# First batch of a fused attention and MLP kernel: where fills, transposes and global queries stand

## The chip, the cores and the metric

The kernel runs on one core of one Trainium2 chip. The metric is the device time of one execution in microseconds (us). Every time of a whole kernel quoted here is a median, with the range beside it where it matters; events within a kernel come from one profiled execution each.

The engines are called PE (TensorE matmul), DVE (VectorE), ACT (ScalarE), Pool (GpSimd) and SP (SyncE, which here only issues loads and stores).

## The reference

Eight batches, eight heads, 512 local and 32 global positions, head size 64. Local queries see a window of 32 positions to each side and the 32 global keys; global queries see everything. The result goes through an MLP with a hard-swish.

```python
k_all = concat([k_g, k_l]);  v_all = concat([v_g, v_l])
out_g = softmax(scale * q_g @ k_all.T) @ v_all
s_l   = concat([scale * q_l @ k_g.T, where(|i-j| <= 32, scale * q_l @ k_l.T, -1e9)])
out_l = softmax(s_l) @ v_all
x = concat([out_g, out_l])  -> 4352 rows x 512
h = x @ w_in;  g = h * clip(h + 3, 0, 6) / 6;  out = g @ w_out
```

## The kernel before

Heads are taken in pairs: four pairs per batch, 32 pairs in all; pairs 0 to 3 are batch 0, pairs 4 to 7 batch 1. A pair goes through these steps. `cast` turns the loaded f32 tiles into f16. `emit_T`, written T(p), transposes q and k on PE and copies them out of PSUM, where PE's results lie. `emit_S`, S(p, 0) and S(p, 1), makes local scores and their exponentials. `emit_SG` and `emit_PG` are the scores and value products of the global queries. `emit_AV` and `emit_X` are the local value products and their transposes. The MLP consists of units: 16 of `u1` per batch (four matmuls with w_in each) and 16 of `u2` (four matmuls with w_out each). `M(n)` issues the next n units.

From batch 2 on, eight units of the batch before fill the gaps of each pair. This change is about what comes before: batch 0, whose weights are still being loaded, and batch 1.

All loads but those of v_g go through 13 staging buffers, used in turn. Such a load can start only when the cast of the tile 13 loads earlier has emptied its buffer.

```python
    NSTG = 13
    def emit_T(p):                       # one PSUM tile for k and q
        psT = ps_tile("psT", FP16)
        for i, t in enumerate((s["kn"], s["qn"])):
            for j in range(NT):
                nc.tensor.matmul(out=psT[:, i * Sl + j * P:...], lhsT=t[:, j], rhs=ident, is_transpose=True)
        nc.vector.tensor_copy(out=kT..., in_=psT[:, 0:Sl]...)
        nc.scalar.copy(out=qT..., in_=psT[:, Sl:2 * Sl]...)
        nc.vector.tensor_copy(out=qT[:, 0:W], in_=qT[:, Sl:Sl + W])
    # ... cut ...
    def first(p):
        cast(p, "k", nc.vector);  cast(p, "qv", nc.gpsimd);  vshift(p, nc.gpsimd)
    first(0); emit_T(0); emit_G(0, 1, "kg"); kglob(0, nc.vector)
    for p in range(NM):                  # NM = 4 pairs of batch 0
        emit_S(p, 0, True)
        if p >= 2: emit_X(p - 2)
        if p + 1 < NM: first(p + 1); emit_T(p + 1)
        if p >= 1: emit_AV(p - 1)
        emit_S(p, 1, True)
    # ... u1 of units 0 to 3, casts of w_in on Pool ...
    nc.gpsimd.memset(qgz, 0.0)           # the fills, all on Pool
    nc.gpsimd.memset(vgs[0], 0.0); nc.gpsimd.memset(vgs[0][rg, :, D:P], 1.0)
    nc.gpsimd.memset(vts[0][:, :, :, D:P], 1.0)
    # ... vgs[0] copy, Eg ...
    for c in range(4, 12): u1(c)
    emit_G(0, 4, "qg"); emit_G(1, 4, "kg")
    for p in range(NM):                  # global queries inside the first MLP
        u1(12 + p); emit_SG(p)
        if p: emit_PG(p - 1)
    emit_PG(NM - 1)
    pin(*ALL)                            # program order up to here, on every engine
    emit_XG(0)
    fill_v(1, nc.gpsimd)                 # ... more fills of batch 1 on Pool ...
    for b in range(1, B): load_vg(b)     # seven v_g loads, issued by Pool
    for i in range(NC): cast_w("out", i, nc.gpsimd)
    kglob(1, nc.gpsimd); vglob(1, nc.gpsimd)
    for p in range(NM, 2 * NM): cast(p, "kqv", nc.gpsimd); vshift(p, nc.gpsimd)
    M(6); emit_T(4); M(1); emit_S(4, 0); M(1); emit_T(5); emit_S(4, 1); emit_SG(4)
```

The softmax here doesn't subtract the row's maximum and nothing guards it: scores larger than these inputs give would overflow.

## Time and profile before

362.3 us (361.7 to 364.3, 4 runs); the profiled execution spans 361.0 us. Four parts of the profile carry the argument. First the page's slices: 40 equal slices of 9 us, each digit the busy share in tenths; PEclk is the granted PE clock in tenths of full speed.

```profile
PE   0778589699999999999999999999999999999994
...
POOL 4756999996840067006710562055300000000000
PEclk9999969589999999999999999999999999999999
DMA  8999299999950669055903590259211000100202
```

From about 100 us on PE is full: it is the bound there, and a pair takes 9.36 us. Before that there are gaps. The stage table gives them in us; its columns are the stretch, its length, busy us (and instructions) of PE, of PE's weight loads, DVE, ACT and Pool, then granted clock, DMA share and GB/s.

```profile
0.00:9.00 9.00, 0.72 (x8) 0.73 (x8) 5.05 (x17) 1.28 (x1) 4.41 (x14) 1.00 0.86 211
...
36.00:45.00 9.00, 4.86 (x25) 2.01 (x22) 7.27 (x9) 4.12 (x6) 8.71 (x13) 0.95 0.22 79
45.00:54.00 9.00, 7.42 (x70) 4.04 (x71) 3.53 (x8) 4.47 (x11) 8.96 (x17) 0.67 0.97 205
...
63.00:72.00 9.00, 5.94 (x59) 3.56 (x59) 6.29 (x12) 5.41 (x11) 8.57 (x15) 0.59 0.96 225
```

In 36 to 45 us Pool is full, the DMA engines do 0.22 of what they could, and PE is half idle. The chain of waits (start, length, what) says why:

```profile
24.62 6.85 DMA stg<-in_moe_w_in_dram
31.52 0.61 POOL win L169
...
32.79 1.75 POOL qgz L464
...
36.05 1.81 POOL vt L467
...
38.98 1.80 POOL vb L418
...
41.06 1.70 POOL vt L484
...
44.40 3.94 POOL vg L150 x7
...
48.39 6.50 POOL wout L169 x12
...
57.98 2.27 POOL vb L145 x4
...
60.88 0.61 POOL kn L136
```

From 31.5 to 61.5 us the chain is one run on Pool: fills from 32.7 to 44.4, v_g issues, w_out casts, copies, then the first casts of batch 1. While the fills run, the full staging buffers of w_out wait for their casts, so no load can start.

Lastly two pairs of lines of the timeline (start, length, engine, line, operation, out<-in; in brackets the idle time before and what ended it). The k and q copies of T(0) don't overlap, and PE waits for the cast of the global queries' rows, which took 2.23 us on DVE:

```profile
9.35 0.69 DVE L215 COPY kT<-psT 128x512 f16<-128x512 f16 x1 [1.13 <-PE psT L209]
10.07 0.58 ACT L218 COPY qT<-psT 128x512 f16<-128x512 f16 x1 [7.97 <-DVE kT L215]
...
41.71 2.23 DVE L185 CAST qgn<-stg 128x512 f16<-128x512 f32 x1
44.00 0.51 PE L188 MATMUL psGT<-ident,qgn 128*128 128x128 f16 x4 [3.65 <-DVE qgn L185]
```

### The profile page before, as it was taken

What the parts mean: (1) busy time and instruction counts of PE and PEld (TensorE: products, weight loads), DVE (VectorE), ACT (ScalarE), POOL (GpSimd) and SP (SyncE); (2) the same over time, 40 slices, a digit from 0 to 9 for tenths busy, and PEclk for the clock granted to TensorE, in tenths of its full rate; (3) what the DMA queues carried; (4) which work ended last, traced back from release to release, by engine and by line L of the source; (5) the groups of instructions that cost most, each with busy time, mean ns of one, the idle gap of its engine ahead of it and who ended that gap; (6) DMA issues with size and microseconds to landing.
All of it is one profiled execution on the core that took longest, in us unless ns stands there. A gap on an engine that the chain in (4) does not pass through costs nothing.

```text
span 361.0 us, 7891 instructions
## 1 busy us (share of the span) xinstructions
PE 331.7 (92%) x3044; PEld 175.4 (49%) x3044; DVE 230.3 (64%) x522; ACT 208.6 (58%) x434; POOL 138.2 (38%) x229
## 2 busy tenths in 40 slices
PE   0778589699999999999999999999999999999994
PEld 0344244355455555555555555555555555544472
DVE  5465832688888468746885589458855786375070
ACT  1464451557885478746874587558845883284170
POOL 4756999996840067006710562055300000000000
PEclk9999969589999999999999999999999999999999
DMA  8999299999950669055903590259211000100202
GB/s 211 335 240 344 74 209 296 224 171 202 192 104 3 146 156 169 2 132 139 197 3 95 139 225 12 59 137 230 44 32 59 31 2 29 60 29 6 84 31 58
DMA packets 103845, 44.29 MB, mean 123 GB/s; under 512 B 91264, under 2 KB 95360, under 8 KB 103808
## 3 DMA queue, kind: packets, MB, share of 16 engines
q1 hardware_dynamic: 101632, 43.53, 51.4%
q0 software_dynamic: 2176, 0.26, 1.2%
q8 instruction: 24, 0.39, 0.5%
q14 instruction: 13, 0.11, 0.1%
HBM read 35.13 MB, written 8.91 MB: 122 GB/s over the span
## 4 chain that ended last, share of the span: by engine, by line
PE 71%; POOL 8%; DVE 6%; DMA 5%; ACT 4%; SPq 3%; issue 1%; POOLq 0%; DVEq 0%; ACTq 0%
PE po L359 30%; PE psH L343 25%; PE psS L243 5%; DMA stg<-in_moe_w_in_dram 4%; PE psT L209 3%; POOL wout L169 2%; DVE E L249 2%; PE psX L316 2%; ACT E L247 2%; SPq L120 2%; PE pav L286 2%; PE pav L283 2%; PE psSG L260 2%; DMA stg<-in_v_l_dram 2%; ACT t L348 1%
## 5 line engine op out<-in xcount | busy, mean ns | idle before, releaser
L359 PE MATMUL po<-wout,gt 128*128 128x512 f16 x544 | 128.1, 382 | 0.0
L343 PE MATMUL psH<-xt,win 128*128 128x512 f16 x512 | 122.0, 384 | 0.6 <-DVE xt L320 0.5
L350 DVE SCALAR_TENSOR_TENSOR gt<-t,psH 128x512 f16<-128x512 f32 (+1 forms) x144 | 90.7, 653 | 30.1 <-ACT t L348 29.1
L348 ACT ACTIVATE t<-psH,half_col 128x512 f32<-128x512 f32 (+1 forms) x144 | 91.5, 669 | 29.7 <-PE psH L343 28.2
L247 ACT ACTIVATE E<-psS 128x512 f16<-128x512 f32 x128 | 70.3, 613 | 22.4 <-PE psS L243 21.9
L343 PEld LDWEIGHTS <-win 128*128 128x128 f16 x576 | 53.1, 98 | 51.2 <-issue 2.4
L359 PEld LDWEIGHTS <-gt 128*128 128x128 f16 x544 | 49.6, 98 | 53.4 <-issue 1.3
L249 DVE TENSOR_TENSOR E<-E,mk 128x512 f16<-128x512 f16 x112 | 55.0, 504 | 29.1 <-ACT E L247 27.1
L145 POOL COPY vb<-vg 32x512 f16<-32x512 f16 x28 | 16.6, 631 | 72.9 <-PE pav L286 72.7
L363 ACT COPY ot<-po 128x512 f32<-128x512 f32 x17 | 10.0, 586 | 57.5 <-PE po L359 57.5
L243 PEld LDWEIGHTS <-kT 64*128 64x128 f16 x512 | 15.5, 97 | 30.4 <-issue 26.0
L243 PE MATMUL psS<-qT,kT 64*128 64x128 f16 x512 | 27.2, 227 | 3.3 <-DVE qT L220 3.2
L320 DVE COPY xt<-psX 128x512 f16<-128x512 f16 x32 | 13.4, 420 | 22.6 <-PE psX L316 22.5
L292 DVE TENSOR_TENSOR xn<-pav,rc 128x256 f16<-128x256 f32 x64 | 26.5, 421 | 1.4
L136 POOL CAST vt<-stg 128x512 f16<-128x512 f32 x32 | 20.4, 638 | 12.3 <-DMA stg<-in_v_l_dram 10.8
L136 POOL CAST qn<-stg 128x512 f16<-128x512 f32 x32 | 20.7, 646 | 7.5 <-DMA stg<-in_q_l_dram 7.0
L136 POOL CAST kn<-stg 128x512 f16<-128x512 f32 x28 | 17.5, 625 | 14.8 <-DMA stg<-in_k_l_dram 13.7
L363 DVE COPY ot<-po 128x512 f32<-128x512 f32 x17 | 11.6, 685 | 17.1 <-PE po L359 17.1
L209 PE MATMUL psT<-ident,kn 128*128 128x128 f16 x128 | 13.2, 228 | 9.6 <-DVE kn L136 9.3
L141 POOL COPY vb<-vt 64x512 f16<-64x512 f16 x32 | 20.7, 646 | 2.1
L224 ACT COPY qT<-psT 128x512 f16<-128x512 f16 x24 | 14.0, 583 | 12.9 <-DVE kT L222 12.9
L286 PE MATMUL pav<-vb,E 128*128 128x65 f16 x256 | 20.2, 195 | 0.0
(76 smaller groups left out, 314.9 us busy)
## 6 DMA issues: line engine op xcount, KB each, us to landing
stg<-in_k_l_dram SPq DMA_DIRECT2D x32, 256.0 KB, 4.8
stg<-in_q_l_dram SPq DMA_DIRECT2D x32, 256.0 KB, 4.9
stg<-in_v_l_dram SPq DMA_DIRECT2D x32, 256.0 KB, 4.9
out_dram<-ot SPq DMA_DIRECT2D x24, 256.0 KB, 2.2
stg<-in_moe_w_in_dram SPq DMA_DIRECT2D x16, 256.0 KB, 5.1
stg<-in_moe_w_out_dram SPq DMA_DIRECT2D x16, 256.0 KB, 5.3
out_dram<-ot SPq DMA_DIRECT2D x8, 192.0 KB, 2.2
out_dram<-ot SPq DMA_DIRECT2D x16, 64.0 KB, 1.9
```

Source lines behind the costliest of these rows:

```text
L136: eng.tensor_copy(out=o, in_=s[c + "f"])
L209: nc.tensor.matmul(out=psT[:, i * Sl + j * P:i * Sl + (j + 1) * P], lhsT=t[:, j], rhs=ident, is_transpose=True)
L243: nc.tensor.matmul(out=pss[e][:, w * P:(w + 1) * P], lhsT=kT[r, c0:c0 + P], rhs=qT[r, w * P:(w + 1) * P], start=not pe_mask, stop=True, sk ...
L247: nc.scalar.activation(out=E[:, ch, e], in_=pss[e], func=EXP, scale=qk_scale)
L249: nc.vector.tensor_tensor(out=E[:, ch, e], in0=E[:, ch, e], in1=mk[:, ch].rearrange("p w c -> p (w c)"), op=mult)
L286: nc.tensor.matmul(out=o, lhsT=E[:, 1, e, w * P:(w + 1) * P], rhs=vb[:, (w - 1) % NT, h, 0:D + 1], start=False, stop=True, skip_group_chec ...
L292: nc.vector.tensor_tensor(out=xn[:, 2 * w2:2 * w2 + 2].rearrange("p w (e d) -> p w e d", e=2), in0=pv[:, :, :, 0:D], in1=rc.to_broadcast([ ...
L343: nc.tensor.matmul(out=ps[:, 0:n], lhsT=w_in_t[m][:, c * P:(c + 1) * P], rhs=rhs(m), start=(m == 0), stop=(m == NM - 1), skip_group_check= ...
L348: nc.scalar.activation(out=t1[:, 0:n], in_=ps[:, 0:n], func=RELU, bias=half_col, scale=1.0 / 6.0)
L350: nc.vector.scalar_tensor_tensor(out=gts[c][:, 0:n], in0=t1[:, 0:n], scalar=1.0, in1=ps[:, 0:n], op0=amin, op1=mult)
L359: nc.tensor.matmul(out=po[t][:, 0:dm], lhsT=gts[c][:, t * P:(t + 1) * P], rhs=w_out_t[c // 4][:, c % 4], start=(c == 0), stop=(c == NC - 1))
L363: (nc.scalar.copy if t % 2 else nc.vector.tensor_copy)(out=ot, in_=po[t][:, 0:dm])
```

## The change

Its intent: take the fills out of Pool's queue, so that w_out and batch 1 are cast as they land; let the copies of q and k overlap by giving each a PSUM bank of its own (a bank is the part of PSUM that one tile fills here); run all transposes of batch 0 as early as the data allows; and put batch 0's global queries behind the w_out casts. The diff, cut to its core:

```diff
-    def emit_T(p):
+    def emit_T(p, qdve=False):
-        psT = ps_tile("psT", FP16)
-        for i, t in enumerate((s["kn"], s["qn"])):
+        ps = {}
+        for c in "kq":
+            ps[c] = ps_tile("psT" + c, FP16)[:, 0:Sl]
             for j in range(NT):
                 ... transposes ...
+        qcopy = nc.vector.tensor_copy if qdve else nc.scalar.copy
@@ loads
     for i in range(NC):
         load_w("in", i)
-        if i == 7:
-            load_g(0, 4, "qg"); load_g(1, 4, "kg")
     for i in range(NC):
         load_w("out", i)
+        if i == 3:
+            load_g(1, 4, "kg"); load_g(0, 4, "qg")
@@ fills: ones_v on ACT, the others on DVE, all but vgs[1]
+    fill_v(0, nc.vector); ones_v(0); nc.scalar.memzero(qgz)
+    cast(0, "k", nc.vector)             # in front of the mask work
     ... mneg built straight from mb, mk later from mneg ...
+    for p in range(1, NM): first(p)     # casts k, q and v, all on Pool
+    for i in range(NC): cast_w("in", i, nc.gpsimd)
+    emit_S(0, 0, True); emit_T(1, True); emit_S(0, 1, True); emit_T(2)
+    emit_S(1, 0, True); emit_S(1, 1, True); emit_AV(0); emit_T(3, True)
+    emit_S(2, 0, True); emit_X(0); ...
     HEAD = 3
     ... u1 of units 0 to 2 spread between AV and X ...
+    fill_vg(0, nc.vector); ... Eg on DVE ...
     for c in range(HEAD, NC): u1(c)     # no global queries in between
     for i in range(NC): cast_w("out", i, nc.gpsimd)
+    emit_G(1, 4, "kg"); emit_G(0, 4, "qg")
+    fill_v(1, nc.vector); fill_vg(1, nc.gpsimd)
     kglob(1, nc.gpsimd); vglob(1, nc.gpsimd)
     for p in range(NM, 2 * NM):
-        cast(p, "kqv", nc.gpsimd); vshift(p, nc.gpsimd)
+        cast(p, "k", nc.vector); cast(p, "qv", nc.gpsimd); vshift(p, nc.gpsimd)
-    M(6); emit_T(4); M(1); emit_S(4, 0); M(1); emit_T(5); emit_S(4, 1); emit_SG(4)
+    M(3); pin(*ALL); emit_T(4); emit_SG(0); emit_SG(1); M(1); emit_SG(2); emit_SG(3)
+    emit_S(4, 0); M(1); (emit_PG of 0 to 3); emit_T(5); emit_S(4, 1)
+    ones_v(1); emit_SG(4); emit_XG(0)
+    for b in range(2, B): load_vg(b)
@@ batch 1's pairs
-        n = (0, 1, 0, 1) if b == 1 else (1, 2, 2, 3)
+        n = (1, 1, 0, 0) if b == 1 else (1, 2, 2, 3)
```

More of the change, by code (lines that the diff above doesn't have):

```diff
@@ L136, in cast, with vshift @@
             eng.tensor_copy(out=o, in_=s[c + "f"])
-    def vshift(p, eng):
+    def vshift(p, eng, n=1):
         b, m = divmod(p, NM)
-        hs = slice(2 * m, 2 * m + 2)
+        hs = slice(2 * m, 2 * m + 2 * n)
         eng.tensor_copy(out=vbs[b % NV][0:D, :, hs, 0:D], in_=vts[b % NV][D:P, :, hs, 0:D])
@@ L201, in kglob @@
                         in_=kgT[:, :, b].unsqueeze(2).to_broadcast([P, NM, NT, Sg]))
-    def emit_T(p):
+    def emit_T(p, qdve=False):
         b, m = divmod(p, NM)
         s = st[p]
-        psT = ps_tile("psT", FP16)
-        for i, t in enumerate((s["kn"], s["qn"])):
-            for j in range(NT):
-                nc.tensor.matmul(out=psT[:, i * Sl + j * P:i * Sl + (j + 1) * P],
-                                 lhsT=t[:, j], rhs=ident, is_transpose=True)
         kT = kTs[b % 2][:, m]
@@ L213, in emit_T @@
         qT = wrk.tile([P, Sl + W], FP16, tag="qT", name="qT", bufs=4)
+        ps = {}
+        for c in "kq":
+            ps[c] = ps_tile("psT" + c, FP16)[:, 0:Sl]
+            for j in range(NT):
+                nc.tensor.matmul(out=ps[c][:, j * P:(j + 1) * P], lhsT=s[c + "n"][:, j], rhs=ident,
+                                 is_transpose=True)
+        qcopy = nc.vector.tensor_copy if qdve else nc.scalar.copy
         if b < NRUN:
@@ L216, in emit_T @@
                 out=kv[:, :, 0:P].rearrange("p u (i j) -> p u i j", j=NT),
-                in_=psT[:, 0:Sl].rearrange("p (j u i) -> p u i j", j=NT, u=NT))
-            nc.scalar.copy(out=qT[:, W:Sl + W].rearrange("p (i j) -> p i j", j=NT),
-                           in_=psT[:, Sl:2 * Sl].rearrange("p (j i) -> p i j", j=NT))
+                in_=ps["k"].rearrange("p (j u i) -> p u i j", j=NT, u=NT))
+            qcopy(out=qT[:, W:Sl + W].rearrange("p (i j) -> p i j", j=NT),
+                  in_=ps["q"].rearrange("p (j i) -> p i j", j=NT))
             nc.vector.tensor_copy(out=qT[:, 0:W], in_=qT[:, Sl:Sl + W])
@@ L222, in emit_T @@
             nc.vector.tensor_copy(out=kv[:, :, 0:P],
-                                  in_=psT[:, 0:Sl].rearrange("p (u c) -> p u c", u=NT))
-            nc.scalar.copy(out=qT[:, W:Sl + W], in_=psT[:, Sl:2 * Sl])
-            nc.scalar.copy(out=qT[:, 0:W], in_=psT[:, 2 * Sl - W:2 * Sl])
+                                  in_=ps["k"].rearrange("p (u c) -> p u c", u=NT))
+            qcopy(out=qT[:, W:Sl + W], in_=ps["q"])
+            qcopy(out=qT[:, 0:W], in_=ps["q"][:, Sl - W:Sl])
         s["qT"], s["kT"] = qT, kT
@@ L394 @@
         load_w("in", i)
-        if i == 7:
-            load_g(0, 4, "qg")
-            load_g(1, 4, "kg")
     for i in range(NC):
         load_w("out", i)
+        if i == 3:
+            load_g(1, 4, "kg")
+            load_g(0, 4, "qg")
     for p in range(NM, 2 * NM + 1):
         load(p)
+    make_identity(nc, ident)
     load_vg(0)
-    make_identity(nc, ident)
     mb = const("mb", [P, 2, P])
-    nc.vector.memset(mb, 1.0)
-    nc.vector.memset(mb[D + Sg:P, 1], 0.0)
-    nc.gpsimd.affine_select(out=mb[:, 0], in_=mb[:, 0], compare_op=is_ge, fill=0.0,
+    ones = const("ones", [P, 1])
+    nc.vector.memset(ones, 1.0)
+    nc.vector.memset(mb, 0.0)
+    nc.vector.memset(mb[D + Sg:P, 1], -30000.0)
+    fill = -30000.0
+    nc.gpsimd.affine_select(out=mb[:, 0], in_=mb[:, 0], compare_op=is_ge, fill=fill,
                             base=0, pattern=[[1, P]], channel_multiplier=-1)
-    nc.gpsimd.affine_select(out=mb[:, 0], in_=mb[:, 0], compare_op=is_ge, fill=0.0,
+    nc.gpsimd.affine_select(out=mb[:, 0], in_=mb[:, 0], compare_op=is_ge, fill=fill,
                             base=2 * W, pattern=[[-1, P]], channel_multiplier=1)
-    nc.gpsimd.affine_select(out=mb[0:D, 1], in_=mb[0:D, 1], compare_op=is_ge, fill=0.0,
+    nc.gpsimd.affine_select(out=mb[0:D, 1], in_=mb[0:D, 1], compare_op=is_ge, fill=fill,
                             base=0, pattern=[[-1, P]], channel_multiplier=1)
@@ L419, in fill_v @@
         eng.memset(vbs[i][0:P - W, :, :, D:D + 1], 1.0)
-    fill_v(0, nc.vector)
-    nc.vector.memset(vts[0][:, :, :, D:D + 1], 1.0)
-    vglob(0, nc.vector)
-    nc.vector.tensor_copy(out=mk, in_=mb.unsqueeze(2).to_broadcast([P, 2, NT, P]))
-    nc.vector.memset(mk[:, 0, 0, 0:W], 0.0)
-    nc.vector.memset(mk[0:D, 1, 0, W:P], 0.0)
-    nc.vector.tensor_scalar(out=mneg, in0=mk.rearrange("p c w q -> p c (w q)"), scalar1=30000.0,
-                            scalar2=-30000.0, op0=mult, op1=mybir.AluOpType.add)
@@ L430, in first, with ones_v, fill_vg @@
-    def first(p):
+        eng.memset(vts[i][:, :, :, D:D + 1], 1.0)
+    def ones_v(i):
+        for u in range(NT):
+            nc.scalar.copy(out=vts[i][:, u, :, D + 1:P],
+                           in_=ones.unsqueeze(2).to_broadcast([P, H, D - 1]))
+    def fill_vg(i, eng):
+        eng.memset(vgs[i], 0.0)
+        eng.memset(vgs[i][rg, :, D:P], 1.0)
+    fill_v(0, nc.vector)
+    ones_v(0)
+    nc.scalar.memzero(qgz)
+    cast(0, "k", nc.vector)
+    mv = mneg.rearrange("p c (w q) -> p c w q", w=NT)
@@ new lines, with first @@
+    nc.vector.tensor_copy(out=mv, in_=mb.unsqueeze(2).to_broadcast([P, 2, NT, P]))
+    nc.vector.memset(mv[:, 0, 0, 0:W], fill)
+    nc.vector.memset(mv[0:D, 1, 0, W:P], fill)
+    def first(p, what="kqv"):
+        cast(p, what, nc.gpsimd)
+        vshift(p, nc.gpsimd)
+    first(0, "qv")
+    load_vg(1)
+    emit_T(0)
+    emit_G(0, 1, "kg")
+    kglob(0, nc.vector)
+    vglob(0, nc.vector)
+    units += moe_units(lambda mm: xts[0][mm], Sl, local_dests(0), early=True)
+    u1 = units.pop(0)
@@ new lines @@
+    for p in range(1, NM):
+        first(p)
+    for i in range(NC):
+        cast_w("in", i, nc.gpsimd)
+    emit_S(0, 0, True)
+    emit_T(1, True)
+    emit_S(0, 1, True)
+    emit_T(2)
+    emit_S(1, 0, True)
+    emit_S(1, 1, True)
+    emit_AV(0)
+    emit_T(3, True)
+    emit_S(2, 0, True)
+    emit_X(0)
+    emit_S(2, 1, True)
+    emit_AV(1)
+    emit_S(3, 0, True)
+    emit_X(1)
+    emit_S(3, 1, True)
+    emit_AV(2)
+    HEAD = 3
+    for c in range(HEAD):
+        u1(c, range(2))
@@ new lines @@
+    emit_X(2)
+    emit_AV(3)
+    for c in range(HEAD):
+        u1(c, range(2, 3))
+    emit_X(3)
+    for c in range(HEAD):
+        u1(c, range(3, 4))
+    fill_vg(0, nc.vector)
+    nc.vector.tensor_copy(out=vgs[0][rg, :, 0:D], in_=vg[rg, 0])
+    for t in Egs:
+        nc.vector.memset(t[:, NT], 0.0)
+    nc.vector.tensor_scalar(out=mk.rearrange("p c w q -> p c (w q)"), in0=mneg, scalar1=-1.0,
+                            scalar2=1.0, op0=is_ge, op1=mult)
+    for c in range(HEAD, NC):
+        u1(c)
@@ L431, in first @@
+    for i in range(NC):
+        cast_w("out", i, nc.gpsimd)
+    emit_G(1, 4, "kg")
+    emit_G(0, 4, "qg")
+    fill_v(1, nc.vector)
+    fill_vg(1, nc.gpsimd)
+    kglob(1, nc.gpsimd)
+    vglob(1, nc.gpsimd)
+    for p in range(NM, 2 * NM):
         cast(p, "k", nc.vector)
@@ L433, in first @@
         vshift(p, nc.gpsimd)
-    first(0)
-    emit_T(0)
-    emit_G(0, 1, "kg")
-    kglob(0, nc.vector)
-    units += moe_units(lambda mm: xts[0][mm], Sl, local_dests(0), early=True)
-    u1 = units.pop(0)
-    for p in range(NM):
-        emit_S(p, 0, True)
-        if p >= 2:
-            emit_X(p - 2)
-        if p + 1 < NM:
-            first(p + 1)
-            emit_T(p + 1)
-        if p >= 1:
-            emit_AV(p - 1)
-        emit_S(p, 1, True)
-    for i in range(4):
-        cast_w("in", i, nc.gpsimd)
-    emit_X(NM - 2)
-    HEAD = 3
-    for c in range(HEAD):
-        u1(c, range(NM - 1))
-    emit_AV(NM - 1)
-    emit_X(NM - 1)
-    for c in range(HEAD):
-        u1(c, range(NM - 1, NM))
-    u1(HEAD)
-    for i in range(4, NC):
-        cast_w("in", i, nc.gpsimd)
-    nc.gpsimd.memset(qgz, 0.0)
-    nc.gpsimd.memset(vgs[0], 0.0)
-    nc.gpsimd.memset(vgs[0][rg, :, D:P], 1.0)
-    nc.gpsimd.memset(vts[0][:, :, :, D:P], 1.0)
-    nc.gpsimd.tensor_copy(out=vgs[0][rg, :, 0:D], in_=vg[rg, 0])
-    for t in Egs:
-        nc.gpsimd.memset(t[:, NT], 0.0)
-    for c in range(4, 12):
-        u1(c)
-    emit_G(0, 4, "qg")
-    emit_G(1, 4, "kg")
-    for p in range(NM):
-        u1(12 + p)
-        emit_SG(p)
-        if p:
-            emit_PG(p - 1)
-    emit_PG(NM - 1)
-    pin(*ALL)
-    emit_XG(0)
-    fill_v(1, nc.gpsimd)
-    nc.gpsimd.memset(vts[1][:, :, :, D:P], 1.0)
-    nc.gpsimd.memset(vgs[1], 0.0)
-    nc.gpsimd.memset(vgs[1][rg, :, D:P], 1.0)
-    for b in range(1, B):
-        load_vg(b)
-    for i in range(NC):
-        cast_w("out", i, nc.gpsimd)
-    kglob(1, nc.gpsimd)
-    vglob(1, nc.gpsimd)
-    for p in range(NM, 2 * NM):
-        cast(p, "kqv", nc.gpsimd)
-        vshift(p, nc.gpsimd)
-    M(6)
+    M(3)
+    pin(*ALL)
     emit_T(4)
-    M(1)
+    emit_SG(0)
+    emit_SG(1)
+    M(1)
+    emit_SG(2)
+    emit_SG(3)
     emit_S(4, 0)
     M(1)
+    for p in range(NM):
+        emit_PG(p)
     emit_T(5)
     emit_S(4, 1)
+    ones_v(1)
     emit_SG(4)
+    emit_XG(0)
+    for b in range(2, B):
+        load_vg(b)
     for p in range(NM, NPAIR):
```

## The prediction

> **What bounds it now.** From about 110 us on TensorE is the bound: the slices show PE at 9 tenths, and the chain of waits runs through psH/po matmuls with a pair every 9.36 us. The loss lies before it: by the stage table PE is busy 0.7 us of the first 9, 4.9 of 36-45, 5.9 of 63-72. In the chain of waits, 31.5 to 61.5 us is one run on Pool: last w_in casts, 11.6 us of fills (qgz, vgs, vt, vb, Eg, 32.7-44.4), 4.0 us of v_g issues, 16 w_out casts (48.4-57.3), 4 us of copies, then the first cast of batch 1 at 60.9. The fills hold the staging buffers: DMA share falls to 0.22 in 36-45, against about 1.0 around it. PE also waits 5.1 us for the two global transposes near 44-46, and the granted clock falls to 0.59. The Trainium skill ("TensorE: Matmul & The Clock Gate", part 1) says that PE's clock is halved after idle windows; the trace agrees.
>
> **What the change does.**
> - Fills leave Pool: about 9 us of the 11.6 go to DVE, Scalar or before the loads; six v_g issues (3.4 us) go behind batch 1's casts; four k casts of batch 1 (2.4 us) go to DVE.
> - k3 was cast on DVE behind attention (21.1 us), which held back w_in's ninth load (issued 20.8) and gave Pool a 3.2 us wait. On Pool at about 14 us it doesn't. k_g/q_g loads move back.
> - q and k transposes share a bank now: the ACT copy starts at 10.07, when the DVE copy (9.35 + 0.69) ends. Own banks let them overlap: about 0.6 us per pair. ("PSUM — Partial Sum Buffer", bank collisions, says that two engines mustn't read one bank together.)
> - k0 is cast before the v_g copies and mask work: T(0) near 5.5-6 us instead of 8.3. Attention still awaits batch 0's last loads (14.9).
> - SG/PG of batch 0 run after T(4): 3 us of PE and ACT work, partly in gaps.
> - u2 units before batch 2 fall from 16 to 13; three (4 x 216 ns each, 2.6 us) go to the PE-bound stage.
>
> **Estimate.** w_in is cast near 28 us (now 32.8), batch 0's u1 ends near 34-37 (now 53), PE then waits for w_out, which comes at about 335 GB/s: cast by about 42 (now 57.3). Then 5 us of fills and copies: q4 cast at 47-48; k7 lands at 47-50, and in DVE's order T(4)'s copy waits for it. It comes near 49, not 62.5: 13 us. Batch 1's iterations stay at about 5 us (DVE: masks, copies), plus about 1 us for SG/PG; pair 8's stage begins near 78-79 instead of 91. Less 2.6 us for the three units: about 10 us net.
>
> Predicted 352.5 us (347 to 358). Faster by over 2%: 0.75; within 2%: 0.24; slower: 0.01.
>
> **Signs.** DMA share near 1 through 36-45; w_out casts end 40-44; T(4)'s kT copy 47-51; k and q copies of one pair overlap; the steady pair still 9.36 us.
>
> **What would make it wrong.** Batch 1's loads or DVE's k casts, in order, stall T(4) past 53; Pool waits for the late v_g loads in front of vglob(2), delaying T(8); staging stalls because k_g/q_g buffers are freed only after u1; delayed SG/PG stretch the batch 1 phase by over 3 us. Each costs 2-4 us. If batch 1's phase shrinks too, the gain is 13 us or more.

## The result

348.6 us (347.6 to 348.7, 4 runs) against 362.3 us. The ratio is 0.961 (95% interval 0.957 to 0.965). A ratio here is the mean time of one kernel's runs over that of the other's of the same rounds, so it is not quite the ratio of the medians. Executions over 1.5% slower than the fastest of the same kernel are left out of the means. The profiled execution spans 346.9 us, 14.1 us less. The slices after:

```profile
PE   1999669989999999999999999999999999999994
...
POOL 5986799988502650076105630355000000000000
PEclk9999767999999999999999999999999999999999
DMA  8998999999406960669025920696011001101102
```

and the same stages:

```profile
0.00:9.00 9.00, 1.90 (x14) 0.99 (x14) 4.24 (x18) 6.90 (x11) 5.13 (x15) 1.00 0.88 214
...
36.00:45.00 9.00, 6.12 (x23) 2.41 (x22) 6.08 (x13) 1.13 (x2) 7.41 (x12) 0.67 1.01 333
45.00:54.00 9.00, 6.07 (x57) 3.62 (x56) 2.75 (x6) 3.65 (x11) 8.55 (x15) 0.69 1.19 277
...
63.00:72.00 9.00, 8.22 (x131) 5.01 (x129) 6.54 (x16) 5.59 (x15) 8.62 (x14) 1.00 0.93 177
```

The hole in the DMA row is gone: 333 GB/s in 36 to 45 us instead of 79. PE's weak stretch moved to 36 to 54 us, at a granted clock of 0.67 and 0.69. The chain of waits in that stretch:

```profile
30.16 7.17 DVE gt L352 x12
...
37.94 0.44 DVE kgn L185
38.40 4.33 DMA stg<-in_moe_w_out_dram
42.77 0.61 POOL wout L169
43.39 0.89 POOL vgs L434
...
45.78 2.25 POOL vb L145 x4
...
48.84 0.62 POOL qn L136
...
49.51 0.62 PE psTq L213 x4
50.15 0.59 ACT qT L220
```

The last w_out load waits for the staging buffer that holds the k_g rows; it is issued at 38.40 us. The first load of batch 1 waits for that of the q_g rows (39.77 us). Both groups of rows are cast on DVE only after the last u1 (37.9 us). After w_out's last landing come Pool's last cast, fill and copies, q of pair 4, and T(4). The timeline around T(4), whose two copies don't overlap, because q is cast late (those of T(5) and T(7) do):

```profile
47.25 0.68 DVE L217 COPY kT<-psTk 128x512 f16<-128x512 f16 x1
47.85 0.46 DVE L136 CAST kn<-stg 128x512 f16<-128x512 f32 x1
...
50.15 0.59 ACT L220 COPY qT<-psTq 128x512 f16<-128x512 f16 x1 [12.84 <-PE psTq L213]
```

To see where the 14.1 us came from, I cut both traces at three events: T(4)'s q copy, T(10)'s k copy (pair 8's iteration begins there), and the transposes of the second group of global rows (pair 10's iteration begins there).

| stretch | before, us | after, us | difference |
|---|---|---|---|
| start to T(4)'s q copy | 63.26 | 50.15 | -13.1 |
| to T(10)'s k copy | 28.27 | 27.49 | -0.8 |
| to the second global transposes | 18.68 | 16.60 | -2.1 |
| to the end | 250.8 | 252.7 | +1.9 |

Most of the gain arises before T(4). How the first two rows share it depends on the mark: cut at T(4)'s k copy (62.53 and 47.25 us), they would be -15.3 and +1.4. The last row is the price of three u2 units that now fall into later batches, less what the split banks save there; a_units below takes the two apart.

### The profile page after: what moved, and what is told of

It reads as the page before. It is cut to its first block, busy times and chain, and to the rows that moved or that the text cites. A ratio compares the mean times of both kernels' runs of the same rounds, so it can differ in the third digit from the quotient of the medians.

```text
span 346.9 us, 7936 instructions
## 1 busy us (share of the span) xinstructions
PE 327.3 (94%) x3044; PEld 174.5 (50%) x3044; DVE 230.9 (67%) x536; ACT 213.9 (62%) x441; POOL 129.5 (37%) x216
## 4 chain that ended last, share of the span: by engine, by line
PE 84%; DVE 7%; ACT 3%; POOL 2%; DMA 1%; issue 1%; POOLq 0%
PE po L361 33%; PE psH L345 31%; PE psS L245 6%; DVE gt L352 3%; PE psX L318 2%; PE psTq L213 2%; PE pav L285 2%; PE psTk L213 2%; PE pav L288 2%; PE psSG L262 2%; PE pg L308 2%; DVE E L251 1%; DMA stg<-in_moe_w_out_dram 1%; ACT vt L430 1%; DVE xn L294 1%; PE psS L239 1%
## 5 line engine op out<-in xcount | busy, mean ns | idle before, releaser
L361 PE MATMUL po<-wout,gt 128*128 128x512 f16 x544 | 131.5, 387 | 0.4 <-DVE kT L224 0.4
L345 PE MATMUL psH<-xt,win 128*128 128x512 f16 x512 | 119.1, 379 | 0.5 <-DVE xt L322 0.5
L350 ACT ACTIVATE t<-psH,half_col 128x512 f32<-128x512 f32 (+1 forms) x144 | 92.1, 665 | 21.6 <-PE psH L345 19.1
L361 PEld LDWEIGHTS <-gt 128*128 128x128 f16 x544 | 50.2, 99 | 54.2 <-issue 4.8
L251 DVE TENSOR_TENSOR E<-E,mk 128x512 f16<-128x512 f16 x112 | 53.6, 496 | 35.5 <-ACT E L249 34.3
L249 ACT ACTIVATE E<-psS 128x512 f16<-128x512 f32 x128 | 69.1, 599 | 10.5 <-PE psS L245 10.2
L226 ACT COPY qT<-psTq 128x512 f16<-128x512 f16 x24 | 14.1, 586 | 36.5 <-PE psTq L213 36.4
L245 PE MATMUL psS<-qT,kT 64*128 64x128 f16 x512 | 25.8, 222 | 0.3 <-DVE qT L222 0.3
L285 PE MATMUL pav<-vt,E 128*128 128x65 f16 x256 | 20.0, 192 | 0.1
L285 PEld LDWEIGHTS <-E 128*128 128x128 f16 x256 | 17.7, 97 | 3.1
```

Of the source, the lines that this page charges most:

```text
L245: nc.tensor.matmul(out=pss[e][:, w * P:(w + 1) * P], lhsT=kT[r, c0:c0 + P], rhs=qT[r, w * P:(w + 1) * P], start=not pe_mask, stop=True, sk ...
L249: nc.scalar.activation(out=E[:, ch, e], in_=pss[e], func=EXP, scale=qk_scale)
L251: nc.vector.tensor_tensor(out=E[:, ch, e], in0=E[:, ch, e], in1=mk[:, ch].rearrange("p w c -> p (w c)"), op=mult)
L285: nc.tensor.matmul(out=o, lhsT=E[:, 0, e, w * P:(w + 1) * P], rhs=vt[:, w, h, 0:D + 1], start=True, stop=False, skip_group_check=True)
L345: nc.tensor.matmul(out=ps[:, 0:n], lhsT=w_in_t[m][:, c * P:(c + 1) * P], rhs=rhs(m), start=(m == 0), stop=(m == NM - 1), skip_group_check= ...
L350: nc.scalar.activation(out=t1[:, 0:n], in_=ps[:, 0:n], func=RELU, bias=half_col, scale=1.0 / 6.0)
```

## The experiments

The theory at the outset was that Pool's queue made the loss and its relief the gain (theory 1). Its rival was that the hoisted transposes and the split banks did it. Twelve kernels ran, all with correct results. They ran in four groups, each with the kernel before beside them (medians 362.1 to 362.7 us), so times of different groups are compared here. Names with u_ undo one part of the changed kernel, b_ add one part to the kernel before, a_ alter the changed kernel. The table gives ratio to the kernel before (interval) and the same events as above, in us of the trace.

| kernel | median us | ratio to before | T(4) q | T(10) k | 2nd global | span |
|---|---|---|---|---|---|---|
| before | 362.3 | 1 | 63.26 | 91.53 | 110.21 | 361.0 |
| changed | 348.6 | 0.961 (0.957-0.965) | 50.15 | 77.64 | 94.24 | 346.9 |
| u_pool | 356.5 | 0.985 (0.982-0.988) | 57.25 | 85.39 | 102.07 | 354.8 |
| u_bank | 353.0 | 0.975 (0.970-0.980) | 51.87 | 79.18 | 96.93 | 350.3 |
| b_fills | 357.8 | 0.990 (0.985-0.994) | 59.98 | 85.90 | 105.01 | 355.8 |
| b_fills_k | 356.9 | 0.986 (0.983-0.989) | 59.14 | 86.33 | 105.03 | 355.8 |
| u_hoist | 348.8 | 0.963 (0.961-0.965) | 50.17 | 77.72 | 94.39 | 347.1 |
| u_glob | 354.6 | 0.979 (0.976-0.982) | 54.88 | 82.96 | 99.63 | 352.3 |
| u_gload | 349.0 | 0.963 (0.959-0.967) | 50.37 | 77.68 | 94.36 | 347.0 |
| b_bank | 358.9 | 0.990 (0.986-0.995) | 61.78 | 87.88 | 106.19 | 356.3 |
| a_sg | 349.4 | 0.966 (0.961-0.970) | 50.89 | 77.49 | 94.11 | 346.8 |
| a_q4 | 350.8 | 0.969 (0.967-0.972) | 50.37 | 78.78 | 95.41 | 348.1 |
| a_best4 | 347.2 | 0.958 (0.954-0.962) | 45.72 | 75.82 | 92.66 | 345.5 |
| a_units | 349.9 | 0.965 (0.962-0.969) | 49.72 | 79.83 | 98.31 | 348.4 |

### u_pool: fills and v_g issues back on Pool

```diff
-    ones_v(0); nc.scalar.memzero(qgz)   # and the DVE fills of vgs[0], Eg, vb[1], the ACT fill of vt[1]
+    nc.gpsimd.memset(qgz, 0.0); fill_vg(0, nc.gpsimd); ...; fill_v(1, nc.gpsimd); ...
+    for b in range(2, B): load_vg(b)
     for i in range(NC): cast_w("out", i, nc.gpsimd)
```

> Changed kernel with the fills (qgz, vgs, vt, vb, Eg) and six v_g issues put back on Pool in front of the w_out casts. Theory 1 (the gain is Pool's queue: fills stood in front of w_out's and batch 1's casts): 15.6 us of Pool work return, 6.6 us of Pool's waits for DMA absorb a part; last w_out cast ends near 53 instead of 43.4, q4 cast near 57 instead of 48.8, time +7 to +9 us, 356 to 358. Rival (the gain is the hoisted first batch and the split banks; Pool has slack now): within 2 us of 348.6.

Measured: 356.5 us, 7.9 us slower than the changed kernel; the last w_out cast ends at 52.2 us instead of 43.4. Theory 1's numbers hold, and 7.1 us of it are there at T(4)'s q copy. The chain of waits runs through the fills again. But 7.9 of about 14 us is not all of the gain.

### b_fills and b_fills_k: the fills alone on the kernel before, then the casts of k1 to k3 on Pool

```diff
-    nc.gpsimd.memset(...)               # the fills of vgs[0], vt, Eg, vb[1]
+    nc.vector.memset(...) / nc.scalar.copy(...)
-    for b in range(1, B): load_vg(b)    # in front of the w_out casts
+    load_vg(1)                          # ... the other six behind batch 1's casts
```
```diff
     def first(p):                       # b_fills_k in addition
-        cast(p, "k", nc.vector)
+        cast(p, "k", nc.gpsimd if p else nc.vector)
```

> Kernel before with only the fills and six v_g issues moved off Pool or behind batch 1's casts. Theory 1: the unbroken Pool run from 31.5 to 61.5 us loses about 13 us, of which DMA (w_out can't land before about 43) takes back 4 to 5: time -7 to -9 us, 353.5 to 355.5. Rival (hoisting and banks made the gain): within 2 us of 362.3.

> As b_fills, and the casts of k1 to k3 on Pool in their order of landing. Theory 1: w_in's ninth load no longer waits for k3's cast behind attention on DVE (3.2 us hole in DMA); w_in and w_out land about 2 to 3 us earlier: a further -2 to -3 us, 351 to 353. Rival: k3's cast is off the chain once the fills are gone: within 1 us of b_fills.

Measured: 357.8 us, only 4.3 us less than before, where 7 to 9 were expected. The w_out casts did end at 46.2 us instead of 57.4, but T(4) did not follow. PE's timeline of b_fills shows the new wait:

```profile
52.56 5.99 PE L359 MATMUL po<-wout,gt 128*128 128x512 f16 x27
58.39 0.39 PE L209 MATMUL psT<-ident,kn 128*128 128x128 f16 x4
```

q of pair 4 was cast at 51.8 us, yet PE reached its transposes at 58.4: the global queries inside u1 and the six w_out units in front of T(4) now stood in the way, in PE's own order. Freed of the fills, Pool was no longer the longest queue. This is why the parts are worth less alone than together.

b_fills_k is another 0.9 us lower, inside the scatter, where 2 to 3 were expected, and its w_in casts end at 33.0 us, as those of b_fills do. SP's queue of b_fills_k shows what holds the ninth w_in load:

```profile
15.67 2.26 SPq L178 DMA_DIRECT2D stg<-in_q_g_dram  x4
18.36 2.13 SPq L178 DMA_DIRECT2D stg<-in_k_g_dram  x3
21.22 4.23 SPq L158 DMA_DIRECT2D stg<-in_moe_w_in_dram  x8
```

The seven small loads take SP from 15.7 to 20.5 us; the profile puts 2.7 us of that down to waits for earlier w_in loads to land. The buffer of k3, cast at 14.4 us, was long free. The prediction had blamed k3's cast; it was wrong there.

### u_bank and b_bank: the banks

```diff
-        ps = {}
-        for c in "kq":
-            ps[c] = ps_tile("psT" + c, FP16)[:, 0:Sl]
+        psT = ps_tile("psT", FP16)      # u_bank; b_bank is the reverse, on the kernel before
+        for i, c in enumerate("kq"):
+            ps[c] = psT[:, i * Sl:(i + 1) * Sl]
```

> Changed kernel with q and k transposes in one bank again, all else kept. Theory 1 (Pool's queue and DMA set the early stage): the copies of a pair run one after the other again, 0.6 us per pair in the seven early pairs, of which little is on the chain: +0.5 to +2 us, 349 to 350.5. Rival (split banks are a main part of the gain): +3 us or more, 351.6 or more, with batch 1's pairs visibly longer. Fewer buffers per pair are used of the seven, which may even help.

> Kernel before with only the q and k transposes in banks of their own. Theory: up to T(4) the chain is Pool's, nothing changes there (kT copy of T(4) at 62 to 63); in batch 1's pairs the two copies overlap, which shortens 62.5 to 91.5 us by 0 to 2 us: 360.3 to 362.3. Rival (u_bank's 4.4 us are the price of the shared bank by itself): 358.5 or less.

Measured: u_bank is 4.4 us slower than the changed kernel, b_bank 3.9 us faster than the kernel run beside it (358.9 against 362.7). Both missed my theory's numbers, in the same direction: u_bank (351.0 to 354.1) fell in the rival's range, b_bank (358.0 to 360.9) just short of it. b_bank is the cleaner of the two, as nothing else moved in its source. Its table row says where: T(4)'s q copy 1.5 us earlier, then 26.1 instead of 28.3 us to T(10), then 18.3 instead of 18.7, then 250.1 instead of 250.8 to the end, where a steady pair takes 9.33 instead of 9.36 us. So the edit is worth about 4 us, spread over the whole kernel. But b_bank is not pure either: up to about 65 us its engines run the instructions of the kernel before in the same order; after that, where the order is not pinned, PE, DVE and ACT run them in another one. Only the 1.5 us before T(4) are the split by itself; how the rest divides between the split and the new order is not shown.

u_bank is not a pure test. Around T(4) the scheduler put the global products of batch 0 in front of k's copy, as I read it because that copy was bound to the late q. Its chain of waits:

```profile
46.65 0.38 ACT Eg L264
...
51.14 0.70 DVE kT L218
51.87 0.59 ACT qT L221
```

In u_bank PE started k's transposes at 46.08 us and q's at 49.42, as q's cast is late on Pool. k's copy starts only at 51.14 us: in DVE's order it now stands behind the global products' result (50.53 us), which itself waited 3.16 us for ACT. In the changed kernel k's copy ran at 47.25, three us ahead of q's. A shared tile thus costs in two ways: the two copies run one after the other, and the earlier operand waits for the later. The second shows by itself in T(0) of u_bank, where the order is that of the changed kernel: k's transposes end at 4.62 us, but the copy starts only after q's.

```profile
5.00 0.61 PE L214 MATMUL psT<-ident,qn 128*128 128x128 f16 x4 [0.38 <-POOL qn L136]
5.65 0.69 DVE L218 COPY kT<-psT 128x512 f16<-128x512 f16 x1 [1.10 <-PE psT L214]
```

In the changed kernel this copy runs at 4.80 us.

### u_hoist: the first batch's order of before

```diff
-    emit_S(0, 0, True); emit_T(1, True); emit_S(0, 1, True); emit_T(2); ...
+    for p in range(NM):                 # the loop of the kernel before, casts still on Pool
+        emit_S(p, 0, True) ... emit_T(p + 1) ... emit_AV(p - 1) ... emit_S(p, 1, True)
```

> Changed kernel with the first batch's order of before (each pair's transposes behind the scores of the pair before, all q copies on Scalar), all else kept. Theory 2 (formed from b_fills, whose chain ran through attention and u1 from 9.5 us on): once Pool is freed, the end of u1 frees the k_g/q_g staging buffers and so lets the last w_out loads start; attention ending 5 to 7 us later costs most of that: +3 to +6 us, 351.5 to 354.5, last early gt near 42 instead of 37.9. Rival (attention is hidden behind w_out's DMA, which ends at 43 anyway): within 1.5 us of 348.6.

Measured: 348.8 us, within 0.2 us of the changed kernel. Attention of batch 0 ended 1.7 us later (X(3)'s copy at 25.78 instead of 24.07 us), and T(4) started where it did. My theory fell; its rival holds: the hoist of the transposes, by itself, is hidden behind the landing of w_out. The seven us by which attention ends earlier than before (31.3 us) come for the larger part from other pieces (the early cast of k0 and the split banks among them); they were not separated further.

### u_glob and u_gload: the global queries and their loads

```diff
+        if i == 7: load_g(0, 4, "qg"); load_g(1, 4, "kg")      # u_gload and u_glob
-    for c in range(HEAD, NC): u1(c)                             # u_glob alone
+    for c in range(HEAD, 12): u1(c)
+    emit_G(0, 4, "qg"); emit_G(1, 4, "kg")
+    for p in range(NM):
+        u1(12 + p); emit_SG(p); ... emit_PG(p - 1)
+    ... emit_XG(0) ...
```

> Changed kernel with batch 0's global queries back inside the first MLP and their loads back behind the eighth w_in load. Theory 2: the seven small loads stand again in the middle of w_in (about 4.5 us of the queue's time against 5 loads' worth), the transposes stop PE, and u1 ends 4 to 6 us later; part of it is hidden while w_out lands, and batch 1's phase is shorter by 1 to 1.5 us: +1 to +4 us. Rival (their place is neutral, as they are the same work): within 1 us.

> Changed kernel with only the seven small k_g/q_g loads put back behind the eighth w_in load; casts, transposes and products of the global queries stay behind the w_out casts. It splits the 6 us of u_glob. If the loads are the cause (w_in's last cast 33 us instead of 27.6): u1 ends 4 to 5 us later, its end comes before the first w_out products, time +4 to +6 us, 352.5 to 354.5. If the place of the products on TensorE is the cause: w_in ends at 33 too, but u1's later end stays hidden behind w_out's loads (which are no later, as the same loads were only moved): within 1.5 us of 348.6. I lean to the second.

Measured: u_glob is 6.0 us slower than the changed kernel, more than theory and rival allowed; u_gload is 0.4 us slower, as I leaned to. Where the loads stand is neutral, although w_in's last cast moves from 27.6 to 33.1 us; PE, DVE, ACT and Pool run their instructions in the order of the changed kernel there, so this is a pure test. Where the products stand is not. In u_glob PE waits 3.0 and 1.5 us for the casts of the two groups of rows, as before the change, and u1 ends at 47.3 us instead of 37.9. The delay reaches T(4) by an indirect way, which the timelines of DVE and Pool show:

```profile
49.22 0.94 DVE L424 MEMSET vb<- 128x1056 uint32 x1 [0.27 <-issue]
...
50.28 2.48 POOL L145 COPY vb<-vg 32x512 f16<-32x512 f16 x4 [4.25 <-issue]
```

The fill of batch 1's vb stands on DVE behind u1; Pool's copy into vb waits for it 4.25 us, and q's cast waits behind that copy. So part of the 6 us belongs to the fill's new place: with this wait removed, PE would still have come to T(4) only at about 51.2 us (its k transposes), where q's followed at 49.5 in the changed kernel. That part of 1.5 to 2 us is worked out, not run; the other 3 us of the 4.7 by which T(4)'s q copy comes later would then be the fill's.

### a_sg, a_q4, a_best4: attempts at a better kernel

```diff
     # a_sg: SG, PG and XG of batch 0 in front of M(3)
     # a_q4: Pool's work for batch 1 in its waits for w_out
     for i in range(NC):
         cast_w("out", i, nc.gpsimd)
+        if i == 3: fill_vg(1, nc.gpsimd)
+        if i == 5: vglob(1, nc.gpsimd)
-    fill_vg(1, nc.gpsimd); kglob(1, nc.gpsimd); vglob(1, nc.gpsimd)
+    kglob(1, nc.vector)
     # a_best4: the same, and
+    fill_v(1, nc.vector)                # at the start of the kernel
+        if c == 10: cast of the k_g rows;  if c == 13: cast of the q_g rows    # between u1 units
+    SG(0..3); M(2); cast(4, "k"); T(4); M(1); PG(0..3); S(4, 0); M(1); cast(5, "k"); T(5); S(4, 1)
+    pin(*ALL); cast(6, "k"); cast(7, "k"); M(1); SG(4); XG(0)
```

> Changed kernel with score and value products of batch 0's global queries in front of the first w_out products (PE idles or runs at a granted clock of 0.67 there, 38 to 49 us), no longer behind T(4). Theory: the copy of T(4)'s q to the first masks of pair 4 loses the four Eg activations (2.4 us on ACT, 50.6 to 53.2 in the chain): -1 to -2.5 us, 346 to 347.5. Rival (pair 4 is bound by the casts on Pool, not by that): within 0.7 us.

> Changed kernel with batch 1's fill of vgs and its v_g copies moved into Pool's waits between w_out casts, kglob(1) on DVE. Theory: chain of the changed kernel ran w_out's last load, Pool 42.8 to 49.5 (cast, fill, copies, q4's cast); 5 us of this leave: q4 cast at 44 to 45, T(4)'s q copy at 45.5 to 46.5 instead of 50.15, time -3 to -4.5 us, 344 to 345.5. Rival (batch 2's loads or Pool later set pair 8's start): -1 us or less.

> Changed kernel mended after a_q4 and a_sg: fill of vb(1) on DVE at the start, fill of vgs(1) and v_g copies of batch 1 between w_out casts, kglob(1) on DVE, k_g/q_g rows cast within u1 (frees their staging buffers before u1's end), batch 0's global scores in front of two w_out products, their value products behind T(4). Theory: q4's cast at 43 to 44.5, T(4)'s q copy at 44.5 to 46.5 instead of 50.15, four Eg activations off the chain: -4 to -6 us, 342.5 to 344.5. Rival (batch 1's phase is held by its own loads and DVE): -1.5 us or less.

a_sg gained nothing (349.4 us). The value products wait for four Eg activations on ACT, and the w_out products stand behind them in PE's order, so these started at 45.5 us and T(4) at 50.2. The four activations left the chain behind T(4) and came back in front of it.

a_q4 lost 2.2 us. I had left the DVE fill of vb behind u1, and Pool's copy into vb, now in the middle of the w_out casts, waited for it:

```profile
40.12 2.66 POOL L145 COPY vb<-vg 32x512 f16<-32x512 f16 x4 [5.29 <-issue]
```

The w_out casts ended at 49.3 us. It is the wait of u_glob again, met a second time.

a_best4 mends both. T(4)'s q copy came at 45.7 us, 4.4 us earlier, as expected. But the time fell only to 347.2 us (346.9 to 348.2, 4 runs), against 348.6 (347.6 to 348.7). The medians differ by 1.4 us; the intervals of the ratios overlap, so it is the fastest kernel seen here but not one shown to be faster. That is its rival's range, not the 4 to 6 us of the theory. The lead shrinks from 4.4 us at T(4) to 1.8 at T(10). In its chain k of pair 5 is cast behind pair 4's masks and an output copy:

```profile
50.28 0.60 DVE ot L373
50.88 0.34 DVE kn L136
```

and Pool again waits for loads of batch 2, 1.0, 0.6 and 1.5 us near 72 to 76 us. Which of the two takes back how much is left open.

### a_units: the three left-over units

```diff
-        n = (1, 1, 0, 0) if b == 1 else (1, 2, 2, 3)
+        n = (1, 1, int(p > NM), 0) if b == 1 else (1, 2, 2, 3)
```

> Changed kernel with the three left-over w_out units of batch 0 done in pairs 5 to 7 (11 units there, 16 in all before pair 8, as before the change). Theory: the prediction's term of 2.6 us for them was wrong, as pairs 8 and 9 wait on ACT and DVE when they begin with the next batch's first products at once, and the left-over units fill that: from T(10)'s kT copy to the transposes of the second global group 18.3 to 19.1 us, as in the kernel before and its variants, instead of 16.8; time within 1 us of 348.6. Rival (work on TensorE is a plain sum there): T(10) to the transposes stays near 16.8 and the time falls by 2 to 2.6 us, to 346 to 346.6.

Measured: 349.9 us (6 runs, 349.1 to 351.7), ratio 0.965. That is 1.3 us above the changed kernel in the medians, 0.3 outside my range, and the intervals of the ratios overlap: not faster, and not shown to be slower. The rival fell. From T(10) to the second global transposes 18.5 us pass, as in the other kernels with 16 units before pair 8 (18.3 to 19.1 us in before, b_fills, b_fills_k, b_bank), where those with 13 units need 16.6 to 17.8. In pairs 5 to 7 the three units weren't free either: T(4) to T(10) took 30.1 us instead of 27.5.

After the second global transposes the units give back what the prediction said: with split banks, kernels with 16 units need 250.1 us to the end (b_bank, a_units), those with 13 need 252.6 to 252.8, which is 2.6 us more. With a shared bank it is 250.8 (before, b_fills, b_fills_k) against 253.4 (u_bank), again 2.6. So the 1.9 us of the table above are 2.6 for the units less 0.7 for the banks.

Why pairs 8 and 9 are shorter with 13 units is shown only in part. About half is where the mark falls: between the two marks PE runs 58 products of 128x512 and 24 of psS in the changed kernel, but 61 and 32 in the kernel before (61 and 30 in a_units), as more of pair 8's work ran ahead of T(10)'s copy. At the 216 and 41 ns from one to the next in the traces, that is an estimated 1.0 of the 2.1 us. The rest goes beyond PE's own work at that rate: in the kernel before, the chain from 91 to 110 us lies by 23% on ACT's `t` and 21% on DVE's `gt`, the two steps behind each product with w_in; in the changed kernel, from 77 to 94 us, 67% is PE's psH. But in b_bank, with 16 units too, most of it is PE's psH as well (71% from 87 to 107 us), and the stretch still takes 18.3 us. So my reason, that pairs 8 and 9 wait on ACT and DVE when they begin with w_in units at once, is not shown.

## Why the prediction came out as it did

The direction, the range and the middle event were right; the size was short by 4 us (10 predicted, 14.1 in the traces). By the prediction's own terms: pair 8's stage was to begin 12 to 13 us earlier and did so 13.9 us earlier; behind T(10) the three units were to cost 2.6 us, but the two rows there sum to -0.2. So 2.8 of the 4 us arose behind T(10), the rest before it. The split banks, worth about 4 us in all, had no term in the sum. Of the signs, DMA share (1.01), last w_out cast (43.4 us) and T(4)'s kT copy (47.25 us) came as forecast; the copies of a pair overlap only in some pairs, and the steady pair takes 9.33 us. Point by point:

- **Pool's run bounds the early stage: right, but not alone.** Undoing the fills costs 7.9 us (u_pool). The rest is other queues: b_fills showed that with the fills gone PE's own order holds T(4) to 58 us.
- **w_out is then limited by DMA, cast by about 42 us: right.** 43.4 us, at 333 GB/s.
- **T(4)'s copy near 49 us instead of 62.5: right in size, partly by luck, with one step wrong.** k's copy ran at 47.25, q's at 50.15. "In DVE's order T(4)'s copy waits for k7" did not happen: k5's cast came after k4's copy. What held T(4) was q's cast behind Pool's fill and copies, and before it the staging buffers of k_g and q_g, which stood among the risks. The wait that was named did not occur; another ended at nearly the same time.
- **"About 0.6 us per pair" for the banks: stated, but left out of the sum.** The split is worth 3.9 us (b_bank) to 4.4 us (u_bank), with a new order of instructions in both. For the eight pairs of batches 0 and 1 the 0.6 us would have made 4.8, but the prediction booked nothing; and it left out that a shared tile ties k's copy to q's transposes.
- **Batch 1's phase, "plus about 1 us": open.** From T(4)'s q copy to T(10) it was 0.8 us shorter; from T(4)'s k copy, which is the 62.5 us that the prediction names, 1.4 us longer. The banks took off 2.2 us there (b_bank); what the global queries put back was not measured by itself.
- **Three units, 2.6 us: the price was right, what came against it was missing.** They cost 2.6 us at the end, but the banks gave 0.7 back there, and pairs 8 and 9 took 2.1 us less, half of it by the place of the mark. a_units moved the units back: T(4)'s q copy to the second global transposes took 4.5 us more, and the whole gained nothing.
- **k3's cast held back w_in: wrong.** SP's own queue with seven small loads did (b_fills_k), and where w_in ends is worth nothing here (u_gload).
- **Global queries: counted as a cost, in truth a gain.** The prediction booked only their work behind T(4). Taking them out of u1 is worth 6.0 us in the changed kernel (u_glob), about 3 us of it through the place of the fill of vb.
- **The hoist**, first in the change's name, is worth 0.2 us, inside the scatter (u_hoist).

The single values add up to more than the whole: 7.9 + 6.0 + 4.4 + 0.4 + 0.2 = 18.9 us against 14. Several queues end near the same time, and undoing any one of them makes it the last.

## What to carry to other kernels

An engine whose queue frees the load buffers sets the pace of the DMA engines, even if its own work looks harmless: put fills, constants and late-needed issues in front of the loads or on idle engines. When one long queue is shortened, look at once for the next that ends near the same time, in the order of the instructions of each engine: a fill or cast moved to another engine can come to stand behind unrelated work there, and two experiments here lost time to exactly that. Operands that become ready at different times should not share a PSUM tile. And the place of a few matmuls is not priced by their own length alone: the three units cost 2.6 us at the end, yet putting them back into the early phase gained nothing.

## What the Trainium skill lacked or had wrong

- "TensorE: Matmul & The Clock Gate", part 1: the table gives "after ≥1 idle window (~3.4µs)" for the slow clock. The kernel before agrees (its clock fell in 44 to 45 us, to a mean of 0.57, after a gap of 3.65 us). The changed kernel shows a case that this row does not cover: its longest gap was 1.85 us, and the clock still fell to one half at 39.0 us, 2.4 us after the last w_in product, as these rows of its stage table show (columns as above). The only PE work in those 2.4 us was one group of transposes (0.34 us). So the clock fell after less than 3.4 us without products, whether transposes count as work or not; why is not shown.

```profile
38.00:39.00 1.00, 0.34 (x4) 0.20 (x4) 0.56 (x3) 0.00 (x0) 0.88 (x3) 1.00 0.97 363
39.00:40.00 1.00, 0.20 (x3) 0.20 (x4) 0.74 (x2) 0.00 (x0) 0.82 (x2) 0.51 1.06 410
```

- "PSUM — Partial Sum Buffer", bank collisions: it tells to keep engines off one bank as a matter of right results. It gives no price of sharing a tile between two readers; here splitting it was worth 3.9 us of 362 (b_bank), the new order of instructions included.
- "GPSIMD Engine Reference", opening: it says that VectorE is about twice as fast at plain elementwise work. The 32x512 copy of v_g rows into vb agrees (0.61 us on Pool, 0.28 us on DVE at the median in the kernel before); the 128x512 cast gained less (0.61 us on Pool, 0.42 us at the fastest on DVE). The fill of vb is no like comparison: it took 1.85 us on Pool as 2112 f16 elements a row and 0.94 us on DVE as 1056 of uint32.
- "SBUF — State Buffer", "Who interferes with whom": it gives the rule that GpSimd and VectorE share a pair of ports as an exclusive lock, so that the one that starts first can block the other for its whole instruction. Beside two slowdowns that it quotes (6.8 and 1.5 times) it has no cost in a whole kernel. Here the same cast of the q_g rows took 2.23 us on DVE while Pool filled vt and vgs, and 0.66 us in the changed kernel beside Pool's casts. This fits the rule, but the cause was not tested by itself.
